# Linear attention and a sentence-level mixture of experts: x kept in the token order of the transposes, output rows put in order by the store

## The chip, the cores and the metric

The kernel runs on one core of one Trainium2 chip. The metric is the device time of one execution in microseconds. The core's engines work side by side, each on its own in-order stream of instructions: TensorE (PE, matrix products, with its weight loads as PEld), VectorE (DVE), ScalarE (ACT), GpSimd (POOL) and SyncE (SP, which here only issues transfers). Sixteen DMA engines move data between memory (HBM) and the on-chip SBUF; matrix products land in PSUM.

## The reference

Eight sentences (B = 8) of S = 576 tokens with 8 heads of 64. Per head a linear attention: q is normalised by a softmax over its 64 features, k by a softmax over the tokens. Then a gate picks one of eight experts for each whole sentence, and the expert's two layers run over all its tokens.

```python
q_s = softmax(q, axis=-1); k_s = softmax(k, axis=2)
kv  = einsum('bhsd,bhse->bhde', k_s, v)
x   = einsum('bhsd,bhde->bhse', q_s, kv)      # then (B, S, H*64), D = 512
logits = x.mean(axis=1) @ w_gate              # (B, 8)
e = argmax(logits); gate = softmax(logits)[e]
out[b] = gate * (relu(x[b] @ w1[e]) @ w2[e])  # w1 512x1024, w2 1024x512
```

## The kernel before

One sentence b is one batch step, in two parts: `attention(b)`, which leaves x transposed in the tile xt (512 features as 4 chunks of 128 partitions, 576 tokens along the free dimension, f16) and the gate, and `moe(b)`, which makes the output rows.

**Loads.** `loads(b)` (L98 to L105) brings q, k and v as two tiles each (i = 0, 1), 576 KB a transfer, from SP's queue, three buffers a name. A partition p of such a tile holds nine consecutive tokens, p * 9 + j with j from 0 to 8.

**Attention.** For each i, ScalarE takes the exponentials (L115, L120), GpSimd casts v (L126), VectorE sums and scales q (L131 to L134). Then PE transposes the nine j blocks of 64 partitions into PSUM (L147), so that column 64 * j + p of the transposed tile is token p * 9 + j, and VectorE copies it to qt (L154). k and v are multiplied (L161), VectorE normalises and masks the product to kv (L168, L170), and for each of the two groups g PE makes 128 features of x for 512 columns (px, L179) and for the other 64 (pxt, L180). VectorE evacuates both with `tensor_tensor_reduce` (L182, L187): it multiplies by ones, writes f16 to xt and adds up each feature for the gate's mean in `pooled`. Its output view `xo` puts the columns into the order of the tokens, so neighbouring elements of an instruction are written nine elements apart. px has one PSUM bank beside the expert's work, so the second group's L179 waits for the first group's L182.

**Gate.** PE multiplies `pooled` with the gate's weights (L195), VectorE finds the expert (L200 to L204), GpSimd reads its number and issues the loads of w1 and w2 (L210 to L216, cast from f32 to f16 on the way, three buffers). L222 to L230 make the gate's value.

**Expert.** `moe(b)` makes eight chunks of the hidden layer (L242 for 512 columns, L247 for 64), evacuated in turn by ScalarE (L252) and VectorE (L254), the 64-column rest by ScalarE (L256). The second layer takes 128 columns of hsb at a time as the stationary side (L263), so that an output tile has one token per partition; the fifth tile has 64. ScalarE scales it by the gate into osb (L268, four buffers), and SP stores it (L269): 128 consecutive rows of `out`, 2 KB each, are 256 KB in one run.

**Sequence.** PE's stream is written by hand: the attention of sentences 0 and 1 comes first, then `moe(b)` step by step with a step of `attention(b + 2)` after each. The other engines' streams are set by the framework's scheduler.

Of the kernel before, what the change touches and what calls it, by code (L numbers as in the profile page):

```python
# [19 lines left out]
def kernel(  # L20
# [12 lines left out]
    nc = tc.nc  # L33

    B, H, S, Dh = q.shape
    D, E = moe_w_gate.shape
    F = moe_w1.shape[2]
    J = S // 64
    SM = 512
    ST = S - SM  # L40
# [27 lines left out]
    ones_f32 = consts.tile([128, 1], FP32)  # L68
# [22 lines left out]
    def pair_src(t, b, i):  # L91

        return t[b].rearrange("(i n g) (p j) d -> i (g p) n (j d)", i=2, n=2, p=64)[i]

    state = {}
    nv = [0]

# [9 lines left out]
    def attention(b, tiles, roomy):  # L107
        xt = xt_pool.tile([128, ND, S], FP16, name="xt")
        pooled = gat_pool.tile([128, ND], FP32, name="pooled")
        x_tag, x_bufs = ("po", 2) if roomy else ("x", 1)  # L110
        t_tag = "hm" if roomy else "tk"
        eqs, eks, vas = [], [], []
        for i in range(2):
            eq = e_pool.tile([128, J, 2, Dh], FP16, name="eq")
            nc.scalar.activation(  # L115
                out=eq.rearrange("p j n d -> p n j d"),
                in_=tiles["q", i].rearrange("p n (j d) -> p n j d", j=J), func=AF.Exp,
            )
            ek = e_pool.tile([128, J, 2, Dh], FP16, name="ek")
            nc.scalar.activation(  # L120
                out=ek.rearrange("p j n d -> p n j d"),
                in_=tiles["k", i].rearrange("p n (j d) -> p n j d", j=J), func=AF.Exp,
            )
            va = v_aug[nv[0] % NVB]
            nv[0] += 1
            nc.gpsimd.tensor_copy(  # L126
                out=va[:, :, 1:].rearrange("p j (n d) -> p n j d", n=2),
                in_=tiles["v", i].rearrange("p n (j d) -> p n j d", j=J),
            )
            qs = stat.tile([128, J, 2], FP32, name="qs")  # L130
            nc.vector.tensor_reduce(out=qs, in_=eq, op=ALU.add, axis=AX.X)  # L131
            qsi = stat.tile([128, J, 2], FP32, name="qsi")
            nc.vector.reciprocal(out=qsi, in_=qs)  # L133
            nc.vector.tensor_tensor(  # L134
                out=eq, in0=eq, in1=qsi.unsqueeze(3).to_broadcast([128, J, 2, Dh]), op=ALU.mult,
            )
            eqs.append(eq)
            eks.append(ek)
            vas.append(va)
        yield  # L140
        for i in range(2):
            eq, ek, va = eqs[i], eks[i], vas[i]
            tps = [bank(t_tag, 2) for g in range(2)]
            for j in range(J):
                for g in range(2):
                    r = slice(64 * g, 64 * g + 64)
                    nc.tensor.transpose(  # L147
                        out=tps[g].bitcast(FP16)[:, 64 * j:64 * j + 64],
                        in_=eq[r, j], identity=ident[r, r],
                    )  # L150
            qts = []
            for g in range(2):
                qt = qt_pool.tile([128, S], FP16, name="qt")
                nc.vector.tensor_copy(out=qt, in_=tps[g].bitcast(FP16)[:, 0:S])  # L154
                qts.append(qt)
            yield
            kps = [bank("tk", 2) for g in range(2)]
            for j in range(J):
                for g in range(2):
                    r = slice(64 * g, 64 * g + 64)  # L160
                    nc.tensor.matmul(  # L161
                        kps[g][:, 0:129], lhsT=ek[r, j], rhs=va[r, j],
                        start=(j == 0), stop=(j == J - 1),
                    )
            kvs = []
            for g in range(2):
                icv = kv_pool.tile([128, 1], FP32, name="icv")
                nc.vector.reciprocal(out=icv, in_=kps[g][:, 0:1])  # L168
                kv = kv_pool.tile([128, 128], FP16, name="kv")
                nc.vector.scalar_tensor_tensor(  # L170
                    out=kv, in0=kps[g][:, 1:129], scalar=icv, in1=blkmask, op0=ALU.mult, op1=ALU.mult,
                )
                kvs.append(kv)
            yield
            for g in range(2):
                c = 2 * i + g
                px = bank(x_tag, x_bufs)
                pxt = kps[g][:, 192:256]
                nc.tensor.matmul(px, lhsT=kvs[g], rhs=qts[g][:, 0:SM], start=True, stop=True)  # L179
                nc.tensor.matmul(pxt, lhsT=kvs[g], rhs=qts[g][:, SM:S], start=True, stop=True)  # L180
                xo = xt[:, c, :].rearrange("q (p j) -> q j p", j=J)
                nc.vector.tensor_tensor_reduce(  # L182
                    out=xo[:, 0:8, :], in0=px.rearrange("q (j p) -> q j p", j=8),
                    in1=ones_f32.unsqueeze(2).to_broadcast([128, 8, 64]),
                    scale=1.0, scalar=0.0, op0=ALU.mult, op1=ALU.add, accum_out=pooled[:, c:c + 1],
                )
                nc.vector.tensor_tensor_reduce(  # L187
                    out=xo[:, 8, :], in0=pxt, in1=ones_f32.to_broadcast([128, ST]),
                    scale=1.0, scalar=pooled[:, c:c + 1], op0=ALU.mult, op1=ALU.add,
                    accum_out=pooled[:, c:c + 1],  # L190
                )
                yield
        pg = bank(x_tag, x_bufs)
        for c in range(ND):
            nc.tensor.matmul(  # L195
                pg[0:1, 0:E], lhsT=pooled[:, c:c + 1], rhs=wg_sb[:, c, :],
                start=(c == 0), stop=(c == ND - 1),
            )
        zz = gat_pool.tile([1, E], FP32, name="zz")
        nc.vector.tensor_copy(out=zz, in_=pg[0:1, 0:E])  # L200
        mx8 = gat_pool.tile([1, 8], FP32, name="mx8")
        nc.vector.max(out=mx8, in_=zz)
        eidx = gat_pool.tile([1, 8], U32, name="eidx")
        nc.vector.max_index(out=eidx, in_max=mx8, in_values=zz)  # L204
        e_val = nc.values_load(eidx[0:1, 0:1], engines=[ET.Pool], min_val=0, max_val=E - 1)
        w1_sb = w_pool.tile([128, ND, F], FP16, name="w1_sb")
        w1_src = moe_w1[ds(e_val, 1)].rearrange("o (i h g e) f -> i h e (o g) f", i=2, h=2, g=2)
        for i in range(2):
            for h in range(2):
                nc.gpsimd.dma_start(  # L210
                    out=w1_sb[64 * h:64 * h + 64, 2 * i:2 * i + 2, :], in_=w1_src[i, h]
                )
        w2_sb = w_pool.tile([128, NF, D], FP16, name="w2_sb")
        w2_src = moe_w2[ds(e_val, 1)].rearrange("o (c p) n -> p (o c) n", p=128)
        nc.gpsimd.dma_start(out=w2_sb[:, 0:4], in_=w2_src[:, 0:4])
        nc.gpsimd.dma_start(out=w2_sb[:, 4:8], in_=w2_src[:, 4:8])  # L216

        nmx = gat_pool.tile([1, 1], FP32, name="nmx")
        nc.vector.tensor_single_scalar(out=nmx, in_=mx8[:, 0:1], scalar=-1.0, op=ALU.mult)
        ex = gat_pool.tile([1, E], FP32, name="ex")  # L220
        sm = gat_pool.tile([1, 1], FP32, name="sm")
        nc.scalar.activation(out=ex, in_=zz, func=AF.Exp, bias=nmx, accum_out=sm)  # L222
        gt = gat_pool.tile([1, 1], FP32, name="gt")
        nc.vector.reciprocal(out=gt, in_=sm)  # L224
        state[b] = [xt, gt, w1_sb, w2_sb]
        yield
        pg2 = bank(x_tag, x_bufs)
        nc.tensor.matmul(pg2[:, 0:1], lhsT=ones_row, rhs=gt, start=True, stop=True)
        gate = gat_pool.tile([128, 1], FP32, name="gate")
        nc.vector.tensor_copy(out=gate, in_=pg2[:, 0:1])  # L230
        state[b][1] = gate
        yield

    def moe(b):
        xt, gate, w1_sb, w2_sb = state.pop(b)
# [23 lines left out]
        for st in range(5):  # L259
            rows = 128 if st < 4 else ST  # L260
            po = bank("po", 2)
            for fc in range(NF):
                nc.tensor.matmul(  # L263
                    po[0:rows], lhsT=hsb[:, fc, st * 128:st * 128 + rows], rhs=w2_sb[:, fc, :],
                    start=(fc == 0), stop=(fc == NF - 1),
                )
            osb = o_pool.tile([128, D], FP32, name="osb")
            nc.scalar.mul(osb[0:rows], po[0:rows], gate[0:rows])  # L268
            nc.sync.dma_start(out=out[b, st * 128:st * 128 + rows, :], in_=osb[0:rows])  # L269
            yield  # L270

    def drain(gen):
# [51 lines left out]
```

The softmax here doesn't subtract the row's maximum and nothing guards it: scores larger than these inputs give would overflow.

## Time and profile before

| | us |
|---|---|
| median of 3 runs | 293.99 (293.45 to 294.01) |
| profiled execution | 294.0 |
| its span | 292.3 |
| PE busy | 194.8 |
| VectorE busy | 180.7 |
| ScalarE busy | 91.5 |
| GpSimd busy | 52.6 |

The span is what the profile shows of one execution, from its first instruction to its last; the execution's own time is 1.7 us longer. Busy time is summed over the instructions of an engine. Because the stages differ, the chain of work that ended last says more: from the last instruction it goes back to what released it, or to the instruction before it on its engine. A row of a group reads: line, engine, operation, output<-input with partitions x elements and type, count, then busy time in total, mean time of one in ns, and idle time of the engine before it with what ended it. SP's "us to landing" is the time from a transfer's issue to its last byte.

### The profile page before, as it was taken

To read this page: it belongs to the slowest core of one execution; us is meant where nothing else is said; L and a number is where in the kernel's file an instruction comes from. 1 tells how busy PE (TensorE), PEld (TensorE's weight loads), DVE (VectorE), ACT (ScalarE), POOL (GpSimd) and SP (SyncE) were. 2 spreads that over 40 slices of the span, in tenths; PEclk is the share of its full clock that TensorE was granted. 3 is DMA by queue.
4 is the path that set the end of the run, shared out by engine and by line. 5 is a ranking of instruction groups with operands and counts; after the bars stand their busy time and mean duration, and the time that the engine had idled before them with its cause. 6 is when DMAs were issued, how large, how long until landed. Compare 5 with 4: busy or idle time off the path is not lost.

```text
span 292.3 us, 4145 instructions
## 1 busy us (share of the span) xinstructions
PE 194.8 (67%) x1552; PEld 97.3 (33%) x1552; DVE 180.7 (62%) x365; ACT 91.5 (31%) x130; POOL 52.6 (18%) x73
## 2 busy tenths in 40 slices
PE   0232233294769566895969585893879675999994
PEld 0111211142434332342424342341434342454441
DVE  2699999758870979259870979259571868030210
ACT  3551241040424323260414323360123102334342
POOL 1411162060104101510104101510004000500000
PEclk9999999997899959996699959998799979999999
DMA  7999999999938996499738910497018900696112
GB/s 251 389 393 392 365 216 272 345 235 291 248 130 154 276 258 214 103 218 285 215 152 145 242 28 0 93 220 137 1 38 165 237 12 36 123 230 171 56 66 96
DMA packets 31956, 54.81 MB, mean 187 GB/s; under 512 B 2752, under 2 KB 10944, under 8 KB 31936
## 3 DMA queue, kind: packets, MB, share of 16 engines
q1 hardware_dynamic: 18304, 37.75, 36.7%
q0 software_dynamic: 13056, 16.78, 35.5%
q8 instruction: 12, 0.20, 0.3%
q10 hardware_dynamic: 576, 0.02, 0.1%
q14 instruction: 8, 0.07, 0.1%
HBM read 61.88 MB, written 9.44 MB: 244 GB/s over the span
## 4 chain that ended last, share of the span: by engine, by line
DVE 52%; PE 42%; DMA 2%; issue 1%; ACT 1%; ACTq 1%; DVEq 0%
DVE xt L182 25%; PE po L263 21%; PE hm L242 14%; DVE eq L134 7%; DVE qs L131 6%; DVE xt L187 5%; DVE hsb L254 4%; DMA wg_sb<-in_moe_w_gate_dram 2%; PE tk L147 2%; DVE kv L170 2%; PE ht L247 1%; PE tk L161 1%; DVE qt L154 1%; DVE qsi L133 1%; ACTq L86 1%
## 5 line engine op out<-in xcount | busy, mean ns | idle before, releaser
L242 PE MATMUL hm<-xt,w_sb 128*128 128x512 f16 x256 | 76.4, 430 | 0.0
L263 PE MATMUL po<-w_sb,hsb 128*128 128x512 f16 (+1 forms) x320 | 73.4, 380 | 0.0
L182 DVE CUSTOM_DVE_ANT_1 xt<-x,ones_f 128x512 f16<-128x512 f32 x24 | 58.8, 2449 | 2.5 <-PE tk L180 2.5
L268 ACT ACTIVATE osb<-po,gate 128x512 f32<-128x512 f32 (+1 forms) x40 | 27.4, 686 | 59.1 <-PE po L263 55.1
L254 DVE TENSOR_SCALAR hsb<-hm 128x512 f16<-128x512 f32 x32 | 24.4, 764 | 32.3 <-PE hm L242 32.0
L263 PEld LDWEIGHTS <-hsb 128*128 128x128 f16 (+1 forms) x320 | 29.9, 100 | 35.0 <-issue 3.4
L210 POOL DMA_DIRECT2D w_sb<-in_moe_w_dram x32 | 19.3, 623 | 109.9 <-DVE gt L224 70.7
L252 ACT ACTIVATE hsb<-hm 128x512 f16<-128x512 f32 x32 | 19.0, 593 | 61.9 <-PE hm L242 61.9
L126 POOL CAST va<-v_in 128x1152 f16<-128x1152 f32 x16 | 20.2, 1272 | 89.8 <-PE tk L161 47.8
L154 DVE COPY qt<-tk 128x576 f16<-128x576 f16 x24 | 9.9, 452 | 40.0 <-PE tk L147 40.0
L242 PEld LDWEIGHTS <-w_sb 128*128 128x128 f16 x256 | 21.9, 104 | 27.1 <-issue 11.5
L179 PE MATMUL x<-qt,kv 128*128 128x512 f16 x24 | 9.4, 391 | 29.6 <-DVE pooled L182 25.7
L131 DVE TENSOR_REDUCE qs<-eq 128x18 f32<-128x1152 f16 x16 | 21.5, 1342 | 7.2 <-ACT eq L115 7.2
L247 PEld LDWEIGHTS <-w_sb 128*128 128x128 f16 x256 | 18.1, 106 | 19.0 <-issue 6.8
L120 ACT ACTIVATE ek<-k_in 128x1152 f16<-128x1152 f32 x16 | 18.5, 1159 | 17.0 <-PE tk L161 16.3
L115 ACT ACTIVATE eq<-q_in 128x1152 f16<-128x1152 f32 x16 | 18.6, 1162 | 16.3 <-PE tk L147 8.1
L161 PE MATMUL tk<-va,ek 64*128 64x129 f16 x288 | 16.0, 272 | 9.2 <-DVE pooled L187 4.7
L134 DVE TENSOR_TENSOR eq<-eq,qsi 128x1152 f16<-128x1152 f16 x16 | 21.7, 1358 | 0.1
L247 PE MATMUL ht<-xt,w_sb 128*128 128x64 f16 x256 | 19.5, 202 | 0.0
L182 DVE CUSTOM_DVE_ANT_1 xt<-po,ones_f 128x512 f16<-128x512 f32 x8 | 18.6, 2512 | 0.7 <-PE po L179 0.4
L187 DVE CUSTOM_DVE_ANT_0 xt<-tk,ones_f,pooled 128x64 f16<-128x64 f32 x32 | 15.9, 513 | 2.2
L161 PEld LDWEIGHTS <-ek 64*128 64x128 f16 x288 | 12.3, 121 | 10.8 <-issue 5.2
(49 smaller groups left out, 122.4 us busy)
## 6 DMA issues: line engine op xcount, KB each, us to landing
q_in<-in_q_dram SPq DMA_DIRECT2D x16, 576.0 KB, 8.0
k_in<-in_k_dram SPq DMA_DIRECT2D x16, 576.0 KB, 9.0
v_in<-in_v_dram SPq DMA_DIRECT2D x16, 576.0 KB, 8.8
w_sb<-in_moe_w_dram POOLq DMA_DIRECT2D x32, 256.0 KB, 7.3
w_sb<-in_moe_w_dram POOLq DMA_DIRECT2D x16, 512.0 KB, 14.5
out_dram<-osb SPq DMA_DIRECT2D x32, 256.0 KB, 4.1
out_dram<-osb SPq DMA_DIRECT2D x8, 128.0 KB, 5.9
wg_sb<-in_moe_w_gate_dram ACTq DMA_DIRECT2D x4, 4.0 KB, 5.4
```

The source lines that it names most:

```text
L126: nc.gpsimd.tensor_copy(out=va[:, :, 1:].rearrange("p j (n d) -> p n j d", n=2), in_=tiles["v", i].rearrange("p n (j d) -> p n j d", j=J),)
L131: nc.vector.tensor_reduce(out=qs, in_=eq, op=ALU.add, axis=AX.X)
L134: nc.vector.tensor_tensor(out=eq, in0=eq, in1=qsi.unsqueeze(3).to_broadcast([128, J, 2, Dh]), op=ALU.mult,)
L161: nc.tensor.matmul(kps[g][:, 0:129], lhsT=ek[r, j], rhs=va[r, j], start=(j == 0), stop=(j == J - 1),)
L182: nc.vector.tensor_tensor_reduce(out=xo[:, 0:8, :], in0=px.rearrange("q (j p) -> q j p", j=8), in1=ones_f32.unsqueeze(2).to_broadcast([128 ...
L187: nc.vector.tensor_tensor_reduce(out=xo[:, 8, :], in0=pxt, in1=ones_f32.to_broadcast([128, ST]), scale=1.0, scalar=pooled[:, c:c + 1], op0 ...
L210: nc.gpsimd.dma_start(out=w1_sb[64 * h:64 * h + 64, 2 * i:2 * i + 2, :], in_=w1_src[i, h])
L242: nc.tensor.matmul(phm, lhsT=w1_sb[:, c, fsl], rhs=xt[:, c, 0:SM], start=(c == 0), stop=(c == ND - 1),)
L247: nc.tensor.matmul(pht[:, fc * ST:(fc + 1) * ST], lhsT=w1_sb[:, c, fsl], rhs=xt[:, c, SM:S], start=(fc == 0 and c == 0), stop=(fc == NF - ...
L254: nc.vector.tensor_single_scalar(out=hsb[:, fc, 0:SM], in_=phm, scalar=0.0, op=ALU.max)
L263: nc.tensor.matmul(po[0:rows], lhsT=hsb[:, fc, st * 128:st * 128 + rows], rhs=w2_sb[:, fc, :], start=(fc == 0), stop=(fc == NF - 1),)
L268: nc.scalar.mul(osb[0:rows], po[0:rows], gate[0:rows])
```

## The change

The columns of xt stay in the order in which the transposes leave them: column 64 * j + p is token p * 9 + j. The two evacuations write contiguously. Everything up to osb works on columns whatever their order; a tile of 128 columns now holds the tokens of two values of j, 64 of each. The store puts them in place: `out_j` views an output sentence as [j, p, d], and tile st stores j = 2 * st and 2 * st + 1, the fifth tile j = 8. A row is still 2 KB; rows that are neighbours in osb are nine rows apart in `out`.

```diff
+    out_j = out.rearrange("b (p j) d -> b j p d", j=J)
...
-                xo = xt[:, c, :].rearrange("q (p j) -> q j p", j=J)
                 nc.vector.tensor_tensor_reduce(
-                    out=xo[:, 0:8, :], in0=px.rearrange("q (j p) -> q j p", j=8),
-                    in1=ones_f32.unsqueeze(2).to_broadcast([128, 8, 64]),
+                    out=xt[:, c, 0:SM], in0=px, in1=ones_f32.to_broadcast([128, SM]),
                     scale=1.0, scalar=0.0, op0=ALU.mult, op1=ALU.add, accum_out=pooled[:, c:c + 1],
                 )
                 nc.vector.tensor_tensor_reduce(
-                    out=xo[:, 8, :], in0=pxt, in1=ones_f32.to_broadcast([128, ST]),
+                    out=xt[:, c, SM:S], in0=pxt, in1=ones_f32.to_broadcast([128, ST]),
...
-            nc.sync.dma_start(out=out[b, st * 128:st * 128 + rows, :], in_=osb[0:rows])
+            js = slice(2 * st, min(2 * st + 2, J))
+            nc.sync.dma_start(out=out_j[b, js], in_=osb[0:rows])
```

No engine's stream gains or loses an instruction or changes its sequence; two kinds of instruction change their shape (lines after the change are two or three further down in the attention, two in the store). The first is on SP, here from its 35th load to the loads of the seventh sentence. Before:

```order
L103 DMA k_in<-in_k_dram 128x2x576
L103 DMA v_in<-in_v_dram 128x2x576
L269 DMA out_dram<-osb 128x512 x4
L269 DMA out_dram<-osb 64x512
L103 DMA q_in<-in_q_dram 128x2x576
L103 DMA v_in<-in_v_dram 128x2x576
```

And now:

```order
L106 DMA k_in<-in_k_dram 128x2x576
L106 DMA v_in<-in_v_dram 128x2x576
L271 DMA out_dram<-osb 2x64x512 x4
L271 DMA out_dram<-osb 64x512
L106 DMA q_in<-in_q_dram 128x2x576
L106 DMA v_in<-in_v_dram 128x2x576
```

The stores stand where they stood, behind the 36 loads of the first six sentences; the four large ones of a sentence have become 2 x 64 rows on the DRAM side, the small one has kept its 64. The second is on VectorE, in the attention beside the first expert (x is the PSUM bank of px, tk that of pxt). Before:

```order
L134 TENSOR_TENSOR eq<-eq,qsi 128x1152
L182 ISA xt,pooled<-x,ones_f_100 128x8x64
L182 ISA pooled 128x1
L254 TENSOR_SCALAR hsb<-hm 128x512
L187 ISA xt,pooled<-tk,ones_f_100,pooled 128x64
L187 ISA pooled 128x1
```

And now:

```order
L137 TENSOR_TENSOR eq<-eq,qsi 128x1152
L184 ISA xt,pooled<-x,ones_f_100 128x512
L184 ISA pooled 128x1
L255 TENSOR_SCALAR hsb<-hm 128x512
L188 ISA xt,pooled<-tk,ones_f_100,pooled 128x64
L188 ISA pooled 128x1
```

The 8 blocks of 64 have become one run of 512; the sequence is as it was.

## The prediction

> **What bounds the kernel now.** I read the chain of work that ended last first, then the groups of instructions on it, then the same chain inside one steady batch, and last the DMA views, because the change touches VectorE's evacuation and the shape of the stores.
>
> ```profile
> DVE 52%; PE 42%; DMA 2%; issue 1%; ACT 1%; ACTq 1%; DVEq 0%
> ...
> L182 DVE CUSTOM_DVE_ANT_1 xt<-x,ones_f 128x512 f16<-128x512 f32 x24 | 58.8, 2449 | 2.5 <-PE tk L180 2.5
> ...
> L254 DVE TENSOR_SCALAR hsb<-hm 128x512 f16<-128x512 f32 x32 | 24.4, 764 | 32.3 <-PE hm L242 32.0
> ...
> L187 DVE CUSTOM_DVE_ANT_0 xt<-tk,ones_f,pooled 128x64 f16<-128x64 f32 x32 | 15.9, 513 | 2.2
> ```
>
> VectorE holds 52% of the chain. Two rows do the same amount of work at very different prices: L182 and L254 both read 128x512 f32 from PSUM and write 128x512 f16, in 2449 ns and 764 ns. L182 writes with a step of nine elements, L254 contiguously; L182 is also a custom operation with an accumulator. From L187 (64 elements, the same step) to L182 (512) the price rises by (2449 - 513) / 448 = 4.3 ns per element.
>
> ```profile
> by line: DVE xt L182 25.2%; PE po L263 20.8%; PE hm L242 14.3%; DVE eq L134 6.5%; DVE qs L131 6.4%; DVE xt L187 4.6%; DVE hsb L254 4.3%; DMA wg_sb<-in_moe_w_gate_dram 2.1%; PE tk L147 2.1%; DVE kv L170 1.9%; issue 1.3%; PE ht L247 1.2%; PE
> ...
> 158.88 0.97 PE hm L242 x4
> ...
> 161.34 0.69 DVE hsb L254
> 162.03 1.26 DVE qs L131
> ...
> 165.28 2.31 DVE xt L182
> ...
> 168.51 2.25 DVE xt L182
> ...
> 170.92 0.50 DVE xt L187
> ...
> 171.48 0.63 PE tk L147 x17
> 172.11 1.84 PE hm L242 x4
> ...
> 191.85 0.97 PE hm L242 x4
> ...
> 254.74 0.97 PE hm L242 x4
> ...
> 271.43 0.97 PE hm L242 x4
> ```
>
> L182 alone is 25.2% of 292.3 us = 73.7 us of the chain, 2.30 us for each of its 32 executions: every one is on it. In the steady batch the transposes of the next pair of heads (L147) start only when the last evacuation is over, so time taken off L182 is time off the batch, as long as nothing else is late. A steady batch, from one first L242 to the next, lasts 191.85 - 158.88 = 33.0 us; one without attention beside it 271.43 - 254.74 = 16.7 us, in which PE never waits.
>
> The DMA side is close behind, and this is where the change can go wrong:
>
> ```profile
> q1 hardware_dynamic: 18304, 37.75, 36.7%
> q0 software_dynamic: 13056, 16.78, 35.5%
> ...
> out_dram<-osb SPq DMA_DIRECT2D x32, 256.0 KB, 4.1
> out_dram<-osb SPq DMA_DIRECT2D x8, 128.0 KB, 5.9
> ```
>
> 36.7 + 35.5 = 72% of the span is packet time on every one of the 16 DMA engines: q1 carries the loads of q, k, v and the stores, q0 the weights.
>
> **How a store is spread now.** Two stretches of the DMA view, first 279 to 292 us (the last batch's five stores and nothing else), then 5 to 35 us (loads alone):
>
> ```profile
> GB/s 0 0 0 0 25 0 0 0 0 0 0 170 397 240 0 0 50 391 353 13 0 0 334 384 88 0 0 208 391 208 0 0 0 6 214 177 6 0 0 0
> DMA packets 657, 1.19 MB, mean 91 GB/s; under 512 B 80, under 2 KB 80, under 8 KB 656
> ## 3 DMA queue, kind: packets, MB, share of 16 engines
> q1 hardware_dynamic: 656, 1.18, 26.0%
> ...
> out_dram<-osb SPq DMA_DIRECT2D x4, 256.0 KB, 2.0
> ```
> ```profile
> DMA packets 5826, 11.71 MB, mean 390 GB/s; under 512 B 752, under 2 KB 752, under 8 KB 5825
> ## 3 DMA queue, kind: packets, MB, share of 16 engines
> q1 hardware_dynamic: 5393, 11.69, 104.6%
> ```
>
> Five stores have 4 x 128 + 64 = 576 rows of 2 KB. The other 80 packets of q1, all under 512 B, are 16 for each store, for the 64-row one too: every store is cut into 16 shares, each with a closing packet. A 256 KB store is therefore 8 rows per engine. 26.0% of 13 us x 16 engines is 54.1 us for 576 rows, 94 ns a row; the best slice, 397 GB/s, gives 2048 B / (397 / 16 GB/s) = 82.5 ns. So such a store takes an engine about 0.7 us.
>
> **The change, part by part.** (1) L182 and L187 write contiguously. Each engine's stream keeps its instructions and their sequence, so nothing is moved or added. The new price of L182 is not in the trace. Low end: 764 ns, the L254 row. High end: 2449 ns, if it is the operation and not the step that costs. I take 764, since L254 has the same size, source and type: 2449 - 764 = 1.685 us, x 32 = 53.9 us off. For L187 the ends are 513 and, from
>
> ```profile
> L170 DVE SCALAR_TENSOR_TENSOR kv<-tk,icv,blkmask 128x128 f16<-128x128 f32 x32 | 8.7, 315 | 0.1
> ```
>
> 315 ns; 4.6% of 292.3 = 13.4 us of it is on the chain, some 28 pieces, 28 x 0.2 = 5.6 us off. A gain larger than these ends is excluded as far as L254 is the cheapest 512-element evacuation of f32 in the page. Taken alone the part would bring 53.9 + 5.6 = 59.5 us.
>
> (2) The matrix products read xt with the same shapes, columns merely permuted: nothing. The position of hsb's columns follows: nothing.
>
> (3) The stores. A 256 KB store had 128 x 512 on both sides and now has 2 x 64 x 512 on the DRAM side; rows stay 2 KB, bytes stay 256 KB. What changes is the count along which shares can be cut. In this trace each issue has a first count of 128 or 64 and is cut into 16 equal shares; a first count of 2 cut along itself can make two shares only. The trace holds no issue with a first count under 16, so the price is bounded from both sides: still 16 shares (8 rows an engine, 0.7 us, as now), or two shares (64 rows on each of two engines, 64 x 82.5 to 94 ns = 5.3 to 6.0 us). **I take two**, because all that the DMA is given anew is that first count, and equal shares along it are what every row so far fits. I also take the same two engines each time: the 32 instructions are alike, and one fixed rule applied to like instructions gives like engines. The fifth store of a batch has 64 rows as its first count and stays on 16.
>
> The Trainium skill says the same in "DMA: Bandwidth & Descriptors", section "Why a DMA increments its semaphore by 16 and not by 1": the engine count is the largest k up to 16 that divides the slowest non-unit dimension of both access patterns, and SP's transfers use the lowest-numbered k engines. By that rule k is 2 and the engines are always the first two; with 16 the sum would be that of the first rival below. No run here shows a k under 16 so far.
>
> The price: these two engines now have a queue of their own length. Per engine over the whole run:
> - loads: 48 x 576 KB = 28.31 MB at 390 GB/s over all 16: 72.6 us (76 us by the 104.6% of packet time);
> - weights: at most 35.5% of 292.3 = 103.8 us of packet time. Where both queues run, packet times overlap:
>
> ```profile
> q0 software_dynamic: 1666, 2.17, 58.1%
> q1 hardware_dynamic: 1900, 4.12, 52.2%
> ```
>
> is 40 to 62 us, 110% of the time. 103.8 / 1.10 = 94 us. Low end, from the weights alone between 231 and 234 us:
>
> ```profile
> DMA packets 621, 0.62 MB, mean 207 GB/s; under 512 B 16, under 2 KB 621, under 8 KB 621
> ```
>
> 2.10 MB a batch / 207 GB/s x 8 = 81 us;
> - 32 stores of 64 rows: 2048 rows x 82.5 to 94 ns = 169 to 192 us, at 88 ns 180 us;
> - 8 stores of 4 rows: 3 us.
>
> Sum: 72.6 + 94 + 180 + 3 = 350 us, with ends at 326 and 375. To this come 0.9 us to the first issue, 2.0 - 0.8 = 1.2 us from the last row to its landing, and 294.0 - 292.3 = 1.7 us that the profiled execution had around its span (it equals the median, 293.99): 3.8 us, together **354 us**.
>
> That sum is the time only if the two engines never run dry. Ahead of the first store SP issues 36 loads (six batches, 54 us of engine time) and POOL two sets of weights (24 us): 78 us, while the first store can come at about 64 us: it starts at 84.2 us in the trace, and 12 of the 32 L182 lie ahead of it, 12 x 1.685 = 20 us.
>
> ```profile
> L269 SPq DMA_DIRECT2D out_dram<-osb x40: 332/333/553, 84.2 to 288.9; - x40
> ```
>
> After that each batch brings 4 x 5.6 = 22.5 us of stores and 12 of weights, for two batches 9 of loads; compute would need about 33.0 - 4 x 1.685 - 0.6 = 26 us a batch. The backlog grows until something waits for it: o_pool has four osb buffers, so the ACTIVATE of L268 waits for the store four before it. Behind it on ScalarE's queue stand the Relu of L252 and L256 and the Exp of L115 and L120; PE waits for their hm and po banks, and VectorE for PE. The evacuation that became cheap then ends earlier in a batch that starts later: the 59.5 us of part 1 are hidden entirely. In the last two batches, without loads or weights, 17 us of PE work meet 22.5 us of stores, so even there the two engines set the end. Idle stretches would add to the sum; I allow 12 us.
>
> **Rivals.**
> 1. *The stores keep their 16 shares* (or four and more). Then the chain above loses 59.5 us: 294 - 59.5 = **235 us**, on the other side. The DMA engines would have 107.3 + 103.8 = 211 us of packet time, 192 with the overlap, below 235. For it: bytes and row length are as before, and the trace never shows fewer than 16 shares. Against it: the first count. The point where it turns: with n engines a store's rows cost each 360 / n us, and 174 + 360 / n meets 294 at n = 3; four would give 264.
> 2. *Two shares, but another pair of engines each time.* Then a store lasts 5.6 us, still inside the 4 x 1.73 us in which four buffers turn (L268 starts 1.73 us apart in the last batch), and no engine has more work than now: about **240 us**. Against it: nothing in the rows rotates.
>
> ```profile
> 281.19 0.69 ACT L268 ACTIVATE osb<-po,gate 128x512 f32<-128x512 f32 x1 [1.18 <-PE po L263]
> ...
> 282.92 0.69 ACT L268 ACTIVATE osb<-po,gate 128x512 f32<-128x512 f32 x1 [1.04 <-PE po L263]
> ```
>
> 3. *The change does nothing*: the custom operation costs 4.3 ns per element in either layout and stores keep 16 shares: **294 us**. With two shares this is the forecast again, since VectorE is then not the bound.
>
> **How the numbers follow.** Two engines, always the same: 82 in 100, 354 us, from 326 + 4 = 330 to 375 + 4 + 12 = 391. Sixteen shares: 11, 235 us. A rotating pair: 4, 240 us. Nothing: 3, 294 us. The range 325 to 392 takes in nearly all of the first case and leaves the others out, 18 to 20 in 100. Faster by over 0.2% (about what a measurement of this kernel can tell from no change) are cases two and three, 0.15; within it most of the last, 0.02; slower 0.83.
>
> **What would show it.** Right: q1 has 18304 - 32 x 14 = 17856 packets (two closing packets instead of 16 for 32 stores); the GB/s row reads near 2 x 25 = 50 where only stores run; stores land after 20 us and more instead of 4.1; ScalarE's L268 waits for the DMA of osb; L182's row near 764 ns although the time grows. Wrong: 18304 packets with landings near 4 us (rival 1), 17856 packets with landings near 7 us (rival 2), L182 near 2449 ns (the price of part 1). If two shares are there but a row takes far from 88 ns, or the two engines run dry, the sum is off by 2.05 us for each ns, or by that idle time.

## The result and the profile after

The changed kernel took 342.75 us (median of 4 runs, 341.65 to 343.21), the kernel before 294.0 us in the same comparison: the ratio is 1.1624, with a 95% interval of 1.1531 to 1.1717. It is slower by 16%. The prediction was 354 us, range 325 to 392.

First the parts of the page that answer to those shown of before: DMA queues (packets, MB, share of 16 engines), the chain that ended last by engine and by line, and two groups on VectorE.

```profile
span 340.0 us, 4144 instructions
...
q1 hardware_dynamic: 17856, 37.75, 31.4%
q0 software_dynamic: 13056, 16.78, 29.3%
...
DMA 48%; DVE 19%; PE 18%; ACT 5%; issue 2%; SPq 1%; ACTq 1%; POOL 0%; DVEq 0%; POOLq 0%
DMA out_dram<-osb 45%; PE hm L243 8%; DVE qs L134 5%; PE po L264 5%; DVE eq L137 4%; DVE xt L184 3%; ACT osb L269 2%; DMA wg_sb<-in_moe_w_gate_dram 2%; DVE hsb L255 2%; ACT eq L118 2%; PE x L182 1%; DMA v_in<-in_v_dram 1%; DVE kv L173 1%; SPq L271 1%; ACT hsb L253 1%
...
L184 DVE CUSTOM_DVE_ANT_0 xt<-x,ones_f 128x512 f16<-128x512 f32 x24 | 16.4, 684 | 6.6 <-PE tk L183 6.6
```

Two things are to be seen. The evacuation did become cheap: L184 takes 684 ns where its forerunner L182 took 2449 ns, and fell from 25.2% of the chain to 3%. But the stores, absent from the named shares of the chain before, now hold 45% of it. The bytes are the same 37.75 MB; the packets of q1 are 448 fewer, 14 for each of the 32 large stores.

The groups by form show the small evacuation, and the DMA view of 312 to 322 us, in the last sentences, shows a stretch in which the stores run alone:

```profile
L188 DVE CUSTOM_DVE_ANT_0 xt<-tk,ones_f,pooled 128x64 f16<-128x64 f32 x32 | 8.8, 281 | 2.2
```
```profile
GB/s 49 49 49 74 25 49 49 57 49 49 49 49 49 49 57 57 49 49 49 49 49 49 49 49 66 49 49 49 49 49 49 49 66 49 49 49 49 49 49 49
DMA packets 248, 0.51 MB, mean 51 GB/s; under 512 B 4, under 2 KB 4, under 8 KB 247
## 3 DMA queue, kind: packets, MB, share of 16 engines
q1 hardware_dynamic: 247, 0.50, 12.8%
```

The stores move 49 GB/s without a break, where before the same stage showed bursts of 397 GB/s between pauses. 12.8% is what two engines of sixteen that never pause would give (2 / 16 = 12.5%). 247 packets less 4 short ones are 243 rows in 12.8% x 10 us x 16 = 20.5 us of engine time: 84 ns a row.

What the engines wait for (us in total, times, longest), and ScalarE's timeline around the first sentence's stores:

```profile
ACT osb L269 <- DMA out_dram<-osb: 120.8, 14, 23.8
...
DVE qs L134 <- ACT eq L118: 64.9, 6, 21.7
PE hm L243 <- ACT hsb L253: 60.9, 7, 20.7
```
```profile
63.94 0.69 ACT L269 ACTIVATE osb<-po,gate 128x512 f32<-128x512 f32 x1 [2.27 <-PE po L264]
...
69.92 0.69 ACT L269 ACTIVATE osb<-po,gate 128x512 f32<-128x512 f32 x1 [1.04 <-PE po L264]
94.37 0.68 ACT L269 ACTIVATE osb<-po,gate 64x512 f32<-64x512 f32 x1 [23.77 <-DMA out_dram<-osb]
94.95 0.58 ACT L253 ACTIVATE hsb<-hm 128x512 f16<-128x512 f32 x1
95.43 1.15 ACT L118 ACTIVATE eq<-q_in 128x1152 f16<-128x1152 f32 x1
```

The fifth tile of sentence 0 needs the first osb buffer again and waits 23.77 us for its store. The Relu and the Exp stand behind it on ScalarE, and for them PE and VectorE wait. The page gives no time to landing for the large stores; on the chain that ended last they stand as eight pieces of 9.8 to 25.8 us, five of them over 20 us.

### The profile page after: what moved, and what is told of

It is laid out like the page before. It is cut to its first block, busy times and chain, and to the rows that moved or that the text cites. A ratio compares the mean times of both kernels' runs of the same rounds, so it can differ in the third digit from the quotient of the medians.

```text
span 340.0 us, 4144 instructions
## 1 busy us (share of the span) xinstructions
PE 193.5 (57%) x1552; PEld 95.5 (28%) x1552; DVE 123.6 (36%) x365; ACT 89.6 (26%) x130; POOL 52.1 (15%) x73
## 3 DMA queue, kind: packets, MB, share of 16 engines
q1 hardware_dynamic: 17856, 37.75, 31.4%
## 4 chain that ended last, share of the span: by engine, by line
DMA 48%; DVE 19%; PE 18%; ACT 5%; issue 2%; SPq 1%; ACTq 1%; POOL 0%; DVEq 0%; POOLq 0%
DMA out_dram<-osb 45%; PE hm L243 8%; DVE qs L134 5%; PE po L264 5%; DVE eq L137 4%; DVE xt L184 3%; ACT osb L269 2%; DMA wg_sb<-in_moe_w_gate_dram 2%; DVE hsb L255 2%; ACT eq L118 2%; PE x L182 1%; DMA v_in<-in_v_dram 1%; DVE kv L173 1%; SPq L271 1%; ACT hsb L253 1%
## 5 line engine op out<-in xcount | busy, mean ns | idle before, releaser
L243 PE MATMUL hm<-xt,w_sb 128*128 128x512 f16 x256 | 74.5, 421 | 60.9 <-ACT hsb L253 60.9
L264 PE MATMUL po<-w_sb,hsb 128*128 128x512 f16 (+1 forms) x320 | 77.8, 393 | 22.9 <-ACT osb L269 22.9
L269 ACT ACTIVATE osb<-po,gate 128x512 f32<-128x512 f32 (+1 forms) x40 | 27.2, 686 | 151.6 <-DMA out_dram<-osb 120.8
L264 PEld LDWEIGHTS <-hsb 128*128 128x128 f16 (+1 forms) x320 | 31.0, 103 | 61.0 <-issue 31.3
L255 DVE TENSOR_SCALAR hsb<-hm 128x512 f16<-128x512 f32 x32 | 22.1, 690 | 44.6 <-PE hm L243 44.0
L184 DVE CUSTOM_DVE_ANT_0 xt<-x,ones_f 128x512 f16<-128x512 f32 x24 | 16.4, 684 | 6.6 <-PE tk L183 6.6
L182 PE MATMUL x<-qt,kv 128*128 128x512 f16 x24 | 10.8, 449 | 11.6 <-DVE kv L173 7.0
L164 PE MATMUL tk<-va,ek 64*128 64x129 f16 x288 | 13.8, 246 | 2.9 <-DVE pooled L188 1.9
L164 PEld LDWEIGHTS <-ek 64*128 64x128 f16 x288 | 10.5, 108 | 4.1 <-issue 2.1
L150 PEld LDWEIGHTS <-eq 64*128 64x128 f16 x288 | 6.4, 103 | 12.6 <-issue 11.8
L182 PE MATMUL po<-qt,kv 128*128 128x512 f16 x8 | 4.4, 612 | 9.3 <-DVE kv L173 9.3
## 6 DMA issues: line engine op xcount, KB each, us to landing
w_sb<-in_moe_w_dram POOLq DMA_DIRECT2D x32, 256.0 KB, 10.6
w_sb<-in_moe_w_dram POOLq DMA_DIRECT2D x16, 512.0 KB, 20.7
```

The costliest lines, as they stand in the source:

```text
L164: nc.tensor.matmul(kps[g][:, 0:129], lhsT=ek[r, j], rhs=va[r, j], start=(j == 0), stop=(j == J - 1),)
L184: nc.vector.tensor_tensor_reduce(out=xt[:, c, 0:SM], in0=px, in1=ones_f32.to_broadcast([128, SM]), scale=1.0, scalar=0.0, op0=ALU.mult, op ...
L243: nc.tensor.matmul(phm, lhsT=w1_sb[:, c, fsl], rhs=xt[:, c, 0:SM], start=(c == 0), stop=(c == ND - 1),)
L255: nc.vector.tensor_single_scalar(out=hsb[:, fc, 0:SM], in_=phm, scalar=0.0, op=ALU.max)
L264: nc.tensor.matmul(po[0:rows], lhsT=hsb[:, fc, st * 128:st * 128 + rows], rhs=w2_sb[:, fc, :], start=(fc == 0), stop=(fc == NF - 1),)
```

## The experiments

Lines of code are those of the changed kernel unless said. The theory: a first count of 2 cuts a store into two shares that always go to the same two engines, and the work of these two sets the end.

**Every store with a first count of 64.** The large store is issued as two:

```diff
-            js = slice(2 * st, min(2 * st + 2, J))
-            nc.sync.dma_start(out=out_j[b, js], in_=osb[0:rows])
+            for h in range(rows // 64):
+                nc.sync.dma_start(out=out_j[b, 2 * st + h], in_=osb[64 * h:64 * h + 64])
```

> The changed kernel, with each large store issued as two stores of 64 rows, so that the first count of every store is 64. Theory (two shares on the same two engines made the stores slow): 16 shares again, q1 has 48*272 + 72*80 = 18816 packets, and the gain of the evacuation shows: 228 to 250 us, likeliest 235. Rival (rows nine apart in HBM are slow to write, whatever the number of shares): near 340 us.

Measured: 250.03 us, ratio to before 0.8488 (0.8449 to 0.8527).

```profile
q1 hardware_dynamic: 18816, 37.76, 45.7%
```

The packets are those of 16 shares. Rows nine apart in memory are not slow: the rival falls. The theory's cause holds, but its 235 us was 15 us too low, and the time lies just past the end of the stated 228 to 250. The waits of this run name the difference:

```profile
DVE qs L134 <- ACT eq L118: 26.3, 3, 19.1
...
ACT osb L269 <- DMA out_dram<-osb: 22.5, 2, 21.1
...
PE hm L243 <- ACT hsb L253: 18.0, 1, 18.0
```

ScalarE's longest wait for a store is 21.1 us, by the timeline from 70 to 92 us. In that stretch the DMA engines are full:

```profile
DMA packets 4531, 7.39 MB, mean 284 GB/s; under 512 B 357, under 2 KB 1908, under 8 KB 4530
...
q0 software_dynamic: 2189, 2.64, 57.3%
q1 hardware_dynamic: 2341, 4.74, 53.6%
...
out_dram<-osb SPq DMA_DIRECT2D x8, 128.0 KB, 12.9
k_in<-in_k_dram SPq DMA_DIRECT2D x1, 576.0 KB, 22.4
v_in<-in_v_dram SPq DMA_DIRECT2D x1, 576.0 KB, 22.6
```

(66 to 92 us of the same run.) The loads of sentence 5, issued just ahead of the first stores on the same queue, need 22 us to land.

**Eight osb buffers, with the stores in two shares and in sixteen.** The edit, once on the changed kernel and once on the kernel of the first experiment:

```diff
-    o_pool = ctx.enter_context(tc.tile_pool(name="o", bufs=4))
+    o_pool = ctx.enter_context(tc.tile_pool(name="o", bufs=8))
```

> The changed kernel with eight osb buffers instead of four. Theory (the work of the two engines sets the end, 72.6 + 94 + 173 + 3 + 3.8 = 346 us with rows of 84 ns): within 2% of the changed kernel's 343 us. Rival (the ring of four buffers leaves the two engines without stores, as between 110 and 120 us and between 155 and 162 us): these stretches go, 320 to 328 us.

Measured: 334.41 us, ratio to before 1.1359 (1.1307 to 1.1412), 2.4% under the changed kernel. This lies between the two, and neither range held: the ring of four costs 8 us, not 18, and the other 40 us over the kernel before stay although the buffers were doubled.

> Stores of 64 rows as in e_split, and eight osb buffers. e_split has one stall that 235 us did not hold: between 70 and 92 us ScalarE waits 21 us for the first store of sentence 0, which lands behind loads of sentence 5 and weights. Theory (the ring of four turns that backlog into a stall of all engines; five tiles of a sentence fit into eight): the stall goes, 230 to 238 us. Rival (the DMA engines are simply full until 92 us and the time comes back as late loads or weights): 246 to 250 us.

Measured: 231.02 us, ratio to before 0.7846 (0.78 to 0.7893), faster than both kernels of this study. The wait for the stores has gone from ScalarE's list:

```profile
  PE po L264: 47.9, 38
  ACT ex L223: 1.6, 2
```

These are all of the waits in front of osb's instructions in that run (us, times). So the stall of the first experiment was the ring of four meeting a stretch of full DMA engines, and its time did not come back elsewhere. From 66 to 92 us the DMA engines move 284 GB/s in both kernels, but PE is busy for 22.8 us of it with eight buffers and for 8.9 us with four. The first rival of the prediction, 235 us, was about right on the chain and had left this stall out. Only about right, because the TensorE clock moved too: it was granted at 0.995 in this run, 0.955 in the first experiment and 0.927 before, and a matrix product of the first layer took 388, 400 and 430 ns in the mean. How much of the gain is the clock's was not separated.

**The store's shape without the faster evacuation.** The kernel before, with only the store's pattern changed:

```diff
-            nc.sync.dma_start(out=out[b, st * 128:st * 128 + rows, :], in_=osb[0:rows])
+            dst = out[b, st * 128:st * 128 + rows]
+            if st < 4:
+                dst = dst.rearrange("(p h) d -> h p d", h=2)
+            nc.sync.dma_start(out=dst, in_=osb[0:rows])
```

> The kernel before with its evacuation nine elements apart, but the 128 rows of each large store handed over as 2 x 64 (every second row), so the rows of a tile land in another sequence. Theory (engine work sets the end): 340 to 352 us, as with the fast evacuation, L182 at 2.4 us. Rival (the ring of four makes each sentence as long as the landing of its first store plus the expert's first layer): the slow evacuation adds some 7 us in each of six sentences, 380 to 390 us. If the shape of the store did nothing: 294 us.

Measured: 346.83 us (one run). L182 is as slow as it was:

```profile
L182 DVE CUSTOM_DVE_ANT_1 xt<-x,ones_f 128x512 f16<-128x512 f32 x24 | 58.7, 2446 | 1.5 <-PE tk L180 1.5
...
q1 hardware_dynamic: 17856, 37.75, 31.1%
```

Together with the first experiment this makes a square of the change's two parts, all with four buffers:

| | first count 128 or 64 | first count 2 |
|---|---|---|
| evacuation nine apart | 294.0 (before) | 346.8 |
| evacuation contiguous | 250.0 | 342.8 (the change) |

With stores on 16 engines the evacuation is worth 44 us; with stores on two it is worth 4 us, which a single run of 346.8 us can't tell from nothing. The shape of the store alone costs 53 us.

**Other first counts.** The changed kernel, the 128 rows of a large store handed over as n blocks (n = 4, then 8):

```diff
-            nc.sync.dma_start(out=out_j[b, js], in_=osb[0:rows])
+            dst = out[b, st * 128:st * 128 + rows]
+            if st < 4:
+                dst = dst.rearrange("(p h) d -> h p d", h=4)
+            nc.sync.dma_start(out=dst, in_=osb[0:rows])
```

> The changed kernel with the 128 rows of each large store handed over as 4 x 32 (every fourth row of the tile's own 128 rows, so the rows land in another sequence). Theory: four shares, q1 has 48*272 + 32*132 + 8*80 = 17920 packets, and the four engines have 72.6 + 94 + 86.5 + 3 + 3.8 = 260 us of work: 245 to 270 us. Rival (any count that isn't a plain run of rows is slow alike): near 340 us.

> The changed kernel with the 128 rows of each large store handed over as 8 x 16 (every eighth row of the tile's own 128 rows, so the rows land in another sequence). Theory: eight shares, 48*272 + 32*136 + 8*80 = 18048 packets on q1; 72.6 + 94 + 43 + 3 + 3.8 = 216 us of work on these engines, no longer the bound: as e_split, 248 to 258 us. Rival (the time depends on whether the pattern is split, not on the count): 281 us or more.

Measured: 280.94 us and 251.93 us (one run each). The packets are 17920 and 18048, n closing ones for each large store:

```profile
q1 hardware_dynamic: 17920, 37.75, 38.8%
```
```profile
q1 hardware_dynamic: 18048, 37.75, 43.7%
```

The time follows the count: 2, 4, 8 and 16 shares give 343, 281, 252 and 250 us, the last two within 1% of each other. The rivals, under which any such pattern would be equally slow, fall. With four shares the sum of engine work, 260 us, was too low by 21 us and the time lay outside the stated 245 to 270 us: work alone isn't the whole of it there. The waits of that run show

```profile
ACT osb L269 <- DMA out_dram<-osb: 57.5, 8, 24.1
```

one of 24.1 us among them, like the stall of the first experiment; that this accounts for the 21 us was not tried.

**The same two engines from another queue?** The second and fourth large store of a sentence issued by ScalarE:

```diff
-            nc.sync.dma_start(out=out_j[b, js], in_=osb[0:rows])
+            (nc.scalar if st % 2 else nc.sync).dma_start(out=out_j[b, js], in_=osb[0:rows])
```

> The changed kernel with the second and fourth large store of a sentence issued by ScalarE instead of SP. Theory (a first count of 2 gives the same two engines whichever queue issues): 335 to 350 us, the sum on the two engines is as before. Rival (each queue has a pair of its own, or ScalarE's transfers start at other engines): four engines share the rows, 275 to 290 us as e_count4.

Measured: 354.30 us (one run), 4 us above the stated bound and 73 us above what four engines give. Half of the large stores moved to the other queue (q10), and nothing was gained:

```profile
q1 hardware_dynamic: 15776, 33.56, 27.7%
q10 hardware_dynamic: 2656, 4.21, 3.2%
...
ACT osb L269 <- DMA out_dram<-osb: 128.5, 13, 32.9
```

The time alone could also come from ScalarE being held up by its own transfers. The DMA view of 333 to 337 us, where rows of both queues are moving and nothing else is, decides it:

```profile
DMA packets 97, 0.20 MB, mean 50 GB/s; under 512 B 0, under 2 KB 0, under 8 KB 97
...
q1 hardware_dynamic: 55, 0.11, 7.2%
q10 hardware_dynamic: 42, 0.09, 5.9%
```

Two queues together move the 50 GB/s that one queue's two-share stores moved, where stores in four shares moved 86 GB/s (267 to 270 us of the run with n = 4). So the two queues' shares meet on the same engines. Why it is 12 us slower than the change itself stays open.

## Why the prediction was right

- **What bounds it.** Right: with stores of 64 rows and eight osb buffers, where no store is waited for, the cheaper evacuation brings 294.0 - 231.0 = 63 us, for the 59.5 us of the prediction (four buffers more and the higher clock included).
- **Part 1, the evacuation.** The price of L182 was taken as 764 ns of L254 and measured 684 ns: 1.765 us off each, for 1.685. So the low end, beyond which the prediction excluded a gain, was not one: 764 ns is a mean, and L254's median before was 692 ns (least 691, most 910). L187 fell by 0.232 us (513 to 281 ns), for 0.2. The step costs, not the operation: L187 and L188 are the same form (CUSTOM_DVE_ANT_0) on the same 64 elements, and differ by 232 / 64 = 3.6 ns per element. (The profile's name for the large one changes from CUSTOM_DVE_ANT_1 to CUSTOM_DVE_ANT_0, so the small pair is the cleaner evidence.)
- **Part 3, two shares.** Right, and the step on which all hung: 17856 packets as stated, 49 GB/s for the stated 50. The rule of the Trainium skill ("DMA: Bandwidth & Descriptors", section "Why a DMA increments its semaphore by 16 and not by 1"), that the engine count is the largest up to 16 that divides the slowest non-unit dimension of both sides, agrees with the trace for 2, 4, 8 and 64: the closing packets of a store are 2, 4, 8 and 16. That SP's shares start at the lowest-numbered engines can't be read here, only that ScalarE's store shares meet SP's.
- **The sum.** Its largest term was mis-sized: a row takes 84 ns, not 88, so 2048 rows are 172 us for 180, which takes 354 us to 346 us. Against the measured 342.75 us that leaves 3 us, and the run with eight buffers shows that two errors cancel there, so the last 3 us of agreement are luck: without the ring of four the time is 334 us, so the work of the two engines is at most that. With 172 us of large stores, 3 of small ones and 3.8 around, loads and weights are at most 155 us of it, where the sum had 167.
- **"The two engines never run dry".** This step was wrong by some 8 us, if the gain of eight buffers is all idle time of the two; the 12 us allowed for it in the range were enough. The views don't name the engine of a packet. Counted from the packets' records, none was under way for 3.3 us in all between the first and the last row stored, and for no time at all with eight buffers, so the rest of the 8 us stays open.
- **What is late next.** Right: L269 waits for osb's stores 120.8 us in total, and the Relu and Exp behind it pass the wait to PE and VectorE. The 59.5 us of the evacuation were hidden but for at most the 4 us of the square above.
- **The rivals.** A rotating pair and the same-as-before case are excluded by the time. The first rival's turning point, n = 3, agrees with the runs: two shares are slower than before, four are faster, though with 281 us for the 264 stated.

## What to carry to other kernels

Before a transfer's access pattern takes over a permutation, look at the first count of both sides as the instruction carries it (here only the DRAM side's was taken below 64): 128 rows as 2 x 64 ran on two engines, the same rows as two transfers of 64 on sixteen, 343 against 250 us. A cheaper step on the chain also brings everything behind it forward; here the stores then met a stretch of full DMA engines, and four more output buffers were worth 19 us. Where a change has two parts, run each alone: this one holds a gain of 44 us and a loss of 53 us, and they don't add up: with the stores on two engines the gain is all but gone.

## What the runs showed of the hardware that was not expected

SP itself is held when it issues a store in two shares behind a backlog. The stores' instructions on SP (duration in ns: least, median, most), before, after, and with stores of 64 rows:

```profile
L269 SPq DMA_DIRECT2D out_dram<-osb x40: 332/333/553, 84.2 to 288.9; - x40
```
```profile
L271 SPq DMA_DIRECT2D out_dram<-osb x40: 509/4932/15887, 70.5 to 325.3; - x40
```
```profile
L271 SPq DMA_DIRECT2D out_dram<-osb x72: 466/467/3719, 70.7 to 245.2; - x72
```

The median issue of the change takes 4.9 us, the longest 15.9 us, where 0.33 us was the rule before; the loads behind such a store on SP's queue wait that long before they are issued at all. Two shares aren't needed for it: the changed kernel's load at 58.5 us, in 16 shares, took 6.1 us to issue where before no load took over 1.3 us, and the first store, its tile ready at 64.6 us, was issued only at 70.5 us. And the stores burden others: the weights' median landing on the page went from 7.3 to 10.6 us and from 14.5 to 20.7 us, and is 8.0 and 14.2 us with stores of 64 rows.

```profile
w_sb<-in_moe_w_dram POOLq DMA_DIRECT2D x32, 256.0 KB, 10.6
w_sb<-in_moe_w_dram POOLq DMA_DIRECT2D x16, 512.0 KB, 20.7
```

From 128 to 132 us of the changed kernel weights and a store are left on about two engines:

```profile
DMA packets 95, 0.15 MB, mean 36 GB/s; under 512 B 1, under 2 KB 47, under 8 KB 95
...
q1 hardware_dynamic: 48, 0.10, 7.2%
q0 software_dynamic: 47, 0.05, 6.9%
```

7.2 + 6.9 = 14% of sixteen engines is little more than two of them, and the two queues take turns, 48 packets to 47. This fits weight shares that stay behind on the two engines of the stores while the other fourteen have finished theirs; that they make up the whole of the later landing isn't shown.
